# Attention feeding a soft mixture of experts: two sums on VectorE change places with a maximum

## Chip, cores and metric

The kernel runs on one core of a Trainium2 chip. The time is device microseconds of one execution; a comparison uses the median of several runs. The engines are named as in the profile: PE is TensorE's matmuls, PEld its weight loads, DVE VectorE, ACT ScalarE, POOL GpSimd, SP SyncE, whose queue issues the DMAs. `L67` stands on every row because one helper records every operation; rows are told apart by the tiles they write and read (`out<-in`).

## What is computed

Causal attention over 8 batches and 12 heads (448 positions, head dimension 64), and its output, one row of 768 numbers for each of 3584 positions, goes through a soft mixture of 8 experts with 4 slots each.

```python
scores = np.where(mask, -1e9, scale * q @ k.T)
attn = np.exp(scores - scores.max(-1)); attn /= attn.sum(-1) + 1e-9
x = attn @ v                                     # all heads side by side: (3584, 768)
logits = x @ phi                                 # (3584, 32)
d = np.exp(logits - logits.max(0)); d /= d.sum(0) + 1e-9
slot_input = d.T @ x                             # "dispatch": over all positions
slot_out[e] = np.maximum(slot_input[e] @ w1[e], 0) @ w2[e]
c = np.exp(logits - logits.max(1)); c /= c.sum(1) + 1e-9
out = c @ slot_out                               # "combine"
```

The maximum over positions and the sum over positions in `d` run over the whole input, so the kernel carries a running maximum, a running sum and a running dispatch result that is rescaled (`si = si * al + new`).

## The kernel before

**Stages.** A head is one of 96, a pair `p` is two heads of one batch, and a batch is six pairs. The main loop has one turn `block(p)` (lines 570 to 677) for each of pairs 0 to 45; line 681 does the last pair in another order; then the rest of the mixture (two weight matrices for each expert, streamed from memory, and the combine) follows as a tail. `a = 2 * p` is the first head of the pair, `m6 = p % 6` the pair's place in its batch.

**One head.** Its scores lie in a PSUM tile `s` of 128 x 1024 fp32, columns given by `SCOL` (line 50): the four blocks of keys start at columns 576, 0, 320 and 512. There are three such tiles, used in turn (`s_[i % 3]`).
- `scores1` (line 259) writes the causal mask by a matmul with the identity (the rows `s<-tri,identb`) and adds the products of q and k. The mask part `c03`, first of all, goes to columns 512 to 703; the part `c12` (256 columns) comes after it.
- `max_keys` (line 289) takes, on DVE, maxima over the keys into the small tile `r`; `max_row(i, 0)` turns them round on PE (`rt`, or `s<-ident,r` when the target is a score tile), and `max_row(i, 1)` (line 319) reduces the turned tile on DVE into `mr`.
- `max_spread` (line 324) spreads `mr` on POOL into the tile `r2` (the rows `r<-mr`).
- `scores2` (line 335), the correction, subtracts the maxima by a matmul with `r2` (the rows `s<-r,k`); it also carries the low parts of q and k, which POOL prepares with two subtractions, `sub_k` (`ks<-kraw,ks`) and `sub_q` (`r<-qraw,qd`).
- `exps` on ACT makes `pt` from the whole tile `s`; `attv_pair` multiplies by v into `po`, and `norm` on DVE divides by the sums and writes `x`.

**One turn.** In PE's order: correction of head a, `scores1` of head a + 2, correction of head a + 1, `scores1` of head a + 3, `attv_pair(p)` with the turning of head a + 2's maxima in its middle, then what the mixture needs, the turning of head a + 3's maxima, and the turning of the pair before's `x` (`xm`). POOL's order in a turn: the spread for head a + 1 (issued at the end of the turn before), `sub_k`, `sub_q`, the spread for head a + 2.

**What the mixture adds.** It uses the free score tile `m = s_[(a + 1) % 3]` (line 649), which the next turn's `scores1` takes again.
- In turns with m6 = 1, 3 or 5 (from p = 3 on) `logits_a` multiplies two pairs' turned `x` by phi into columns 0 to 127, and `logits_t` (line 444) adds that to the running tile `lt` on DVE (`lt<-s,lt`, `lt<-s,mk`).
- In turns with m6 = 3, 4 or 0 (from p = 9 on) `dispatch_a` multiplies a finished batch's `x` by its weights `gs` into 128 columns from 512, 256 columns from 512, or 384 columns from 0, and `dispatch_b` (line 486) adds that to `si` on DVE (`si<-si,al,s`), scaled by `al`, which ACT makes in the turn with m6 = 3.
- In turns with m6 = 2 `logits_e` copies two tiles out on DVE (`gs<-s`, `lg<-s`).
- In every turn the second head's maxima are turned into the last 128 columns of the same tile, 896 to 1023 (line 664), and reduced from there (`mr<-s`).

**Order of the work.** It is written by hand. Every operation goes through the helper `_InOrder` (line 57), which keeps each engine's instructions in the order of the program; between engines the framework puts the waits that the tiles ask for. So what stands behind a waiting instruction on its engine waits too.

Of the kernel before, what the change touches and what calls it, by code (L numbers as in the profile page):

```python
# [17 lines left out]
P = 128  # L18
# [64 lines left out]
def attention_soft_moe(ctx: ExitStack, tc: tile.TileContext, qk, va, phi, w, out):  # L83
# [52 lines left out]
    def loads_v(p, eng=nc.sync):  # L136
        if p < NPAIR:
            eng.dma_start(out=va_[p % 2], in_=va[p])
# [30 lines left out]
    def load_w(n):  # L169
        if n < len(order):  # L170
            t = wtiles[order[n]] = slot(n, f"w{n}")
            q, g, c = place(n), (n + 2) // 4, WN * ((n + 2) % 4)
            if n < RES or n == NBUF or q >= RES + LATE2:
                nc.sync.dma_start(out=t, in_=w[g, :, c:c + WN])
            elif 4 <= q < RES and n > NBUF:
                if q % 4 == 3:
                    nc.sync.dma_start(out=group(n), in_=w[g])
            elif n % 2:
                t = group(n)
                nc.sync.dma_start(out=t[:, 2 * WN:] if q < RES else t, in_=w[g, :, c - WN:c + WN])  # L180
# [39 lines left out]
    def misc(name):  # L220
        return ps_1.tile([P, 512], F32, tag="m", name=name)
# [13 lines left out]
    def cast_q(p, hs=slice(0, 2)):  # L235
        if p < NPAIR:
            nc.scalar.activation(out=qd[:, hs], in_=st["raw", 0, p][:, hs], func=AF.Copy)
# [10 lines left out]
    def copy_k2(p, hs=slice(0, 2)):  # L248
        if p < NPAIR:
            nc.scalar.activation(out=heads(k2_)[64:P, hs, 0:S], in_=kv(p)[0:64, hs],  # L250
                                 func=AF.Copy)
# [58 lines left out]
    def max_row(i, k, w=RW - RF, to=None):  # L310
        if i >= NHD:
            return
        if k == 0:
            st["rt", i] = misc(f"rt{i}") if to is None else to
            if w == AW:
                nc.tensor.matmul(st["rt", i][0:w, 0:P], r_[i % 2][:, RF:RF + w], ident, start=True, stop=True)
            else:
                nc.tensor.transpose(out=st["rt", i][0:w, 0:P], in_=r_[i % 2][:, RF:RF + w], identity=ident)
        else:
            mr = st["mr", i] = wk.tile([NQB, 32], F32, tag="mr", name=f"mr{i}", bufs=2)  # L320
            nc.vector.tensor_reduce(out=mr, in_=st.pop(("rt", i))[0:NQB, 0:P].rearrange("p (g t)->p t g", g=4),
                                    axis=AX.X, op=ALU.max, negate=True)
# [12 lines left out]
    def scores2(i, cs):  # L335
        if i >= NHD:
            return
        p, h = divmod(i, 2)
        s = st["s", i]
        k2 = k2_  # L340
        for c in cs:
            o, w, m = KS * h + P * c, S - CQ0[c], min(P, KS - P * c)
            nc.tensor.matmul(s[0:m, SCOL[c]:SCOL[c] + w], k2[:, o:o + m],
                             r2[:, h, CQ0[c]:S], start=False, stop=True, skip_group_check=True)

    def exps(i):
        if i < NHD:
            nc.scalar.activation(out=pt_[i % 2][:, 0:1024], in_=st.pop(("s", i)), func=AF.Exp, scale=SCALE)
# [56 lines left out]
    def norm(p, k):  # L405
        if k == 0:
            sm = st["sm", p] = moe.tile([P, NQ], F32, tag="sm", name=f"sm{p}", bufs=2)
            nc.vector.tensor_scalar(out=sm, in0=po2[:, :, HD], scalar1=EPS, scalar2=None, op0=ALU.add)
        elif k == 1:
            nc.vector.reciprocal(out=st["sm", p], in_=st["sm", p])  # L410
        else:
            x, sm = x_of(p), st.pop(("sm", p))
            m = NCH - 1
            nc.vector.tensor_tensor(out=x[:, 0:m].rearrange("p c (h d)->p h c d", h=2),
                                    in0=po2[:, 0:2 * m, 0:HD].rearrange("p (h c) d->p h c d", h=2),
                                    in1=sm[:, 0:2 * m].rearrange("p (h c)->p h c", h=2).unsqueeze(3)
                                    .to_broadcast([P, 2, m, HD]), op=ALU.mult)
            for h in range(2):
                a = AW * h
                nc.vector.tensor_scalar(out=x[0:AW, m, HD * h:HD * h + HD], in0=po2[a:a + AW, 2 * m, 0:HD],  # L420
                                        scalar1=sm[a:a + AW, 2 * m:2 * m + 1], scalar2=None, op0=ALU.mult)
# [22 lines left out]
    def logits_t(j, g):  # L444

        nc.vector.tensor_tensor(out=lt, in0=g, in1=lt if j else mk, op=ALU.add)
# [39 lines left out]
    def dispatch_b(b, hf, sp, sl=slice(0, 384)):  # L486
        s = si[:, 384 * hf + sl.start:384 * hf + sl.stop]
        nc.vector.scalar_tensor_tensor(out=s, in0=s, scalar=st["al", b][:, 0:1], in1=sp[:, 0:sl.stop - sl.start],
                                       op0=ALU.mult, op1=ALU.add)
# [80 lines left out]
    def block(p):  # L570
        a, b = 2 * p, p // 6 - 1
        m6 = p % 6
        if p + 1 < NPAIR:
            loads_v(p + 1, nc.sync if p + 1 < NPAIR - 1 else nc.scalar)
        if p % 2 and p < 44 or p in (16, 30):
            load_w(st["w"])
            st["w"] += 1

        if p:
            norm(p - 1, 2)  # L580
        scores2(a, range(NCH))
        exps(a)
        if p == 0:
            copy_k2(0, h1)
            cast_q(1, h1)
            warm(START[3], pob)
            max_row(1, 0)
            max_row(1, 1)
            max_spread(1)
            sub_k(1, h1, nc.vector)  # L590
        elif p > 1:
            xcopy(p - 2)
        scores1_all(a + 2)
        if p == 0:
            warm(START[2], pob)
        for k in range(3):
            max_keys(a + 2, k)
        if p == 0:
            cast_k(2, h0)
        scores2(a + 1, range(NCH))  # L600
        exps(a + 1)
        if p == 0:
            cast_k(2, h1)
        scores1_all(a + 3)
        if m6 == 2 and p > 6:
            logits_b(b)
        max_keys(a + 3, 0)
        late_k = p == 1
        if p == 1:
            sub_q(2, h0)  # L610
            sub_k(3, h0)
            sub_q(2, h1)
            load_qk(4, 0)
        elif p:
            sub_k(p + 2, h0 if late_k else slice(0, 2))
            if not late_k:
                load_qk(p + 4, 1)
            sub_q(p + 1)
            load_qk(p + 3, 0)
        else:  # L620
            sub_q(1, h0)
            sub_q(1, h1)
            load_qk(3, 0)
            sub_k(2, h0)
        copy_k2(p + 1)
        if m6 == 2 and p > 6:
            logits_d(b, lt)
        if p:
            cast_k(p + 3)
            cast_q(p + 2)  # L630
        else:
            cast_q(2)
            cast_k(3)
        if m6 == 3 and p > 6:
            logits_al(b)
        elif m6 == 4 and p > 6:
            logits_n(b)
        attv_pair(p)
        max_row(a + 2, 1)
        max_spread(a + 2)  # L640
        if p == 0:
            sub_k(2, h1)
            load_qk(4, 1)
        for k in (1, 2):
            max_keys(a + 3, k)
        for k in range(2):
            norm(p, k)

        m = s_[(a + 1) % 3]
        parts = []  # L650
        if m6 in (1, 3, 5) and p > 1:
            j = (m6 + 3) % 6
            logits_a(b if m6 == 1 else p // 6, (j, j + 1), m[:, 0:P])
        elif m6 == 2 and p > 6:
            logits_e(b, m, 0)
        if m6 == 3 and p > 6:
            parts = [(b, 0, slice(0, P), 512)]
        elif m6 == 4 and p > 6:
            parts = [(b, 0, slice(P, 3 * P), 512)]
        elif m6 == 0 and p > 6:  # L660
            parts = [(b - 1, 1, slice(0, 3 * P), 0)]
        for d, hf, sl, o in parts:
            dispatch_a(d, hf, m[:, o:o + sl.stop - sl.start], sl)
        max_row(a + 3, 0, to=m[:, 1024 - P:1024])
        max_row(a + 3, 1)
        if m6 == 2 and p > 6:
            logits_e(b, m, 1)
        max_spread(a + 3)
        if late_k:
            sub_k(p + 2, h1)  # L670
            load_qk(p + 4, 1)
        if m6 in (1, 3, 5) and p > 1:
            logits_t(j, m[:, 0:P])
        for d, hf, sl, o in parts:
            dispatch_b(d, hf, m[:, o:o + sl.stop - sl.start], sl)
        if p:
            xtrans(p - 1)

# [7 lines left out]
    i, b, p = NHD - 1, NB - 1, NPAIR - 1  # L686
# [62 lines left out]
    parts = [(hf, slice(a, a + 192)) for hf in range(2) for a in (0, 192)]  # L749
# [256 lines left out]
```

## Time and profile before

| | us |
|---|---|
| median of 3 runs (lowest, highest) | 396.44 (396.0, 397.08) |
| the profiled execution's own time | 395.86 |
| its span in the trace | 394.1 |
| main loop and last pair, up to about | 302 |
| tail (experts and combine) | 92 |

PE is busy 365.4 us of the span, DVE 294.9, ACT 283.0, POOL 256.6 (all of POOL's work lies in the loop). The granted TensorE clock is full in the loop. One cycle of six turns, a batch, takes 36.2 to 36.3 us. A row of the timeline reads: start, duration, engine, line, operation, tiles out<-in, shapes, count, and in brackets the engine's idle time before it with what ended it by the profile. A row with a count over 1 is several instructions merged, with the time from the first's start to the last's end. A matmul row gives the modelled end. The instruction named after an arrow is the one that ended last by the profile and need not be the one that was waited for.

### The profile page before, as it was taken

The numbers are of one execution on the slowest core, as the hardware profiler recorded it, in microseconds if no ns is written. First come the engines' busy times: TensorE is split into PE (matmuls) and PEld (weight loads), VectorE is DVE, ScalarE is ACT, GpSimd is POOL, SyncE is SP. The second block draws the span as 40 slices with busy tenths as digits, with TensorE's granted clock in tenths as the row PEclk, the third lists the DMA queues.
The fourth block names the chain that finished last, engine by engine and source line by source line (L and its number), as shares of the span: only waits on it lengthen the run. The fifth ranks groups of instructions, "written<-read, shape, count | busy, mean of one in ns | idle before, by whom it ended". The sixth has DMA issues, their size and how long they took to land.

```text
span 394.1 us, 14000 instructions
## 1 busy us (share of the span) xinstructions
PE 365.4 (93%) x5766; PEld 293.3 (74%) x5766; DVE 294.9 (75%) x835; ACT 283.0 (72%) x397; POOL 256.6 (65%) x214
## 2 busy tenths in 40 slices
PE   7899999999999999999999999999999998997840
PEld 3689889888988998898889888988986544533420
DVE  7787889888888888898888988888885575433540
ACT  5888889888898898888988989888864011432430
POOL 5998889888898888898988988889861000000000
PEclk9999999999999999999999999999999999999995
DMA  7858887778898788787987876887579999999997
GB/s 259 306 194 283 293 285 247 254 256 276 286 312 275 239 276 284 254 248 266 318 308 235 307 238 244 279 283 258 176 250 374 414 438 425 429 423 415 430 433 324
DMA packets 28720, 119.17 MB, mean 302 GB/s; under 512 B 3440, under 2 KB 3952, under 8 KB 26480
## 3 DMA queue, kind: packets, MB, share of 16 engines
q1 hardware_dynamic: 28512, 118.01, 82.9%
q8 instruction: 45, 0.74, 0.7%
q10 hardware_dynamic: 144, 0.27, 0.2%
q14 instruction: 19, 0.16, 0.1%
HBM read 107.25 MB, written 11.01 MB: 300 GB/s over the span
## 4 chain that ended last, share of the span: by engine, by line
PE 64%; DMA 11%; POOL 9%; DVE 6%; ACT 4%; issue 2%; SPq 0%; POOLq 0%; DVEq 0%; ACTq 0%
PE s L67 35%; PE po L67 20%; DMA w<-in_w_dram 9%; POOL r L67 6%; PE xm L67 4%; POOL ks L67 3%; DVE lm L67 2%; PE rt L67 2%; DMA kraw<-in_qk_dram 2%; DVE lg L67 1%; ACT qd L67 1%; PE pp L67 1%; PE e L67 1%; DVE si L67 1%; ACT w L67 1%
## 5 line engine op out<-in xcount | busy, mean ns | idle before, releaser
L67 DVE TRANSPOSE_TENSOR_REDUCE r<-s 128x32 f32<-128x1024 f32 x96 | 119.5, 1245 | 7.4 <-PE s L67 4.7
L67 ACT ACTIVATE pt<-s 128x1024 f32<-128x1024 f32 x96 | 98.7, 1029 | 30.8 <-PE s L67 22.5
L67 PEld LDWEIGHTS po<-va,pt 128*64 128x64 f32 x3040 | 103.6, 138 | 12.0 <-issue 11.5
L67 PE MATMUL po<-va,pt 128*64 128x65 f32 x3040 | 110.6, 224 | 0.0
L67 POOL TENSOR_TENSOR r<-qraw,qd 64x896 fp32r<-64x896 f32 (+1 forms) x49 | 99.3, 2027 | 3.2 <-ACT qd L67 1.8
L67 POOL TENSOR_TENSOR ks<-kraw,ks 64x896 fp32r<-64x896 f32 (+1 forms) x48 | 89.7, 1870 | 4.1 <-ACT ks L67 0.4
L67 POOL TENSOR_SCALAR_AFFINE_SELECT r<-mr 14x448 fp32r<-14x448 f32 x96 | 61.8, 644 | 31.9 <-DVE mr L67 27.2
L67 PE MATMUL s<-qd,ks 128*66 128x64 f32 (+3 forms) x384 | 80.2, 320 | 0.0
L67 PE MATMUL s<-r,k 128*128 128x448 f32 (+3 forms) x384 | 65.1, 291 | 3.1 <-POOL r L67 3.1
L67 PEld LDWEIGHTS s<-r,k 128*128 128x128 f32 (+1 forms) x384 | 59.3, 175 | 8.8 <-POOL r L67 6.6
L67 PEld LDWEIGHTS s<-qd,ks 128*128 128x128 f32 (+1 forms) x384 | 52.1, 182 | 2.0 <-issue 0.9
L67 ACT ACTIVATE ks<-kraw 128x896 fp32r<-128x896 f32 (+1 forms) x49 | 45.0, 920 | 5.3 <-DMA kraw<-in_qk_dram 4.1
L67 ACT ACTIVATE k<-ks 64x896 fp32r<-64x896 f32 (+1 forms) x49 | 45.8, 935 | 1.2
L67 ACT ACTIVATE qd<-qraw 128x896 fp32r<-128x896 f32 (+1 forms) x48 | 44.7, 931 | 1.3 <-POOL r L67 0.7
L67 PE MATMUL s<-tri,identb 128*128 128x192 bf16 x192 | 39.2, 268 | 0.6
L67 DVE TENSOR_REDUCE r<-r 128x16 f32<-128x32 f32 x192 | 33.7, 176 | 5.0
L67 DVE TENSOR_REDUCE mr<-s 14x32 f32<-14x128 f32 x47 | 13.1, 279 | 21.9 <-ACT qd L67 14.1
L67 PE MATMUL xm<-ident,x 128*128 128x128 f32 x188 | 28.3, 273 | 0.0
L67 ACT ACTIVATE xts<-xm 128x512 f32<-128x512 f32 x46 | 27.1, 590 | 0.0
L67 DVE TENSOR_SCALAR x<-po,sm 64x64 f32<-64x64 f32 x94 | 26.0, 276 | 0.7
L67 DVE TENSOR_TENSOR x<-po,sm 128x384 f32<-128x384 f32 x47 | 25.2, 537 | 0.0
L67 DVE COPY w<-pp 128x384 f32<-128x384 f32 x28 | 14.4, 553 | 13.2 <-PE pp L67 13.1
(148 smaller groups left out, 393.6 us busy)
## 6 DMA issues: line engine op xcount, KB each, us to landing
w<-in_w_dram SPq DMA_DIRECT2D x34, 768.0 KB, 6.6
kraw<-in_qk_dram SPq DMA_DIRECT2D x46, 448.0 KB, 4.3
qraw<-in_qk_dram SPq DMA_DIRECT2D x46, 448.0 KB, 4.5
w<-in_w_dram SPq DMA_DIRECT2D x5, 3072.0 KB, 23.9
va<-in_va_dram SPq DMA_DIRECT2D x47, 260.0 KB, 4.9
out_dram<-w SPq DMA_DIRECT2D x7, 1536.0 KB, 13.3
w<-in_w_dram SPq DMA_DIRECT2D x5, 1536.0 KB, 9.9
qk<-in_qk_dram SPq DMA_DIRECT2D x2, 448.0 KB, 7.2
```

The costliest lines, as they stand in the source:

```text
L67: return self._tc.keep_in_program_order(op(*args, **kwargs))
```

## The change

In `block(p)`, two calls move up on DVE: `logits_t` (m6 = 1, 3, 5) and `dispatch_b` (m6 = 3, 4, 0) are called between the turning of the second head's maxima on PE and their reduction on DVE, where they were called behind that reduction and its spread. No operation is added or dropped.

```diff
         for d, hf, sl, o in parts:
             dispatch_a(d, hf, m[:, o:o + sl.stop - sl.start], sl)
         max_row(a + 3, 0, to=m[:, 1024 - P:1024])
+        if m6 in (1, 3, 5) and p > 1:
+            logits_t(j, m[:, 0:P])
+        for d, hf, sl, o in parts:
+            dispatch_b(d, hf, m[:, o:o + sl.stop - sl.start], sl)
         max_row(a + 3, 1)
         if m6 == 2 and p > 6:
             logits_e(b, m, 1)
@@
         if late_k:
             sub_k(p + 2, h1)
             load_qk(p + 4, 1)
-        if m6 in (1, 3, 5) and p > 1:
-            logits_t(j, m[:, 0:P])
-        for d, hf, sl, o in parts:
-            dispatch_b(d, hf, m[:, o:o + sl.stop - sl.start], sl)
         if p:
             xtrans(p - 1)
```

## The prediction

> **What bounds the kernel now.** I read the page first, then the waits, then the engines' timelines over one full cycle of six turns of the loop (a turn is one call of `block(p)`; turns 22 to 27 start at 143.2, 149.3, 155.3, 161.4, 167.6 and 173.3 us).
>
> ```profile
> PE 365.4 (93%) x5766; PEld 293.3 (74%) x5766; DVE 294.9 (75%) x835; ACT 283.0 (72%) x397; POOL 256.6 (65%) x214
> ```
> ```profile
> POOL r L67 <- DVE mr L67: 27.2, 41, 1.2
> ```
>
> TensorE (PE) is busy 93% of the span, so the loop can only get longer through a wait of PE. The second row says where PE's nearest rival sits: GpSimd (POOL) spends its idle time waiting for the maxima `mr` that VectorE (DVE) makes, 27.2 us in 41 waits. One turn of POOL, turn 25:
>
> ```profile
> 161.70 0.64 POOL L67 TENSOR_SCALAR_AFFINE_SELECT r<-mr 14x448 fp32r<-14x448 f32 x1 [0.68 <-DVE mr L67]
> 162.42 1.94 POOL L67 TENSOR_TENSOR ks<-kraw,ks 64x896 fp32r<-64x896 f32 x1
> 164.33 2.11 POOL L67 TENSOR_TENSOR r<-qraw,qd 64x896 fp32r<-64x896 f32 x1
> 166.51 0.64 POOL L67 TENSOR_SCALAR_AFFINE_SELECT r<-mr 14x448 fp32r<-14x448 f32 x1
> ```
>
> After its one wait POOL has no gap over 0.1 us. It spreads the second head's maxima (161.70), does the two subtractions, and spreads the next first head's maxima (166.51 to 167.15). So if the spread at 161.70 starts late, the one at 166.51 is late by as much. PE needs both: the first for the second correction of that turn, the second for the first correction of the next turn.
>
> **The change, part by part.** Nothing is added or removed. On DVE the logits sum `lt` (turns with p mod 6 = 1, 3, 5) and the dispatch sum `si` (p mod 6 = 3, 4, 0) go from behind `mr` to in front of it. PE, ACT, POOL and SP keep their order and no DMA is moved. DVE now, at the ends of turns 21, 22 and 24:
>
> ```profile
> 143.16 0.28 DVE L67 TENSOR_REDUCE mr<-s 14x32 f32<-14x128 f32 x1 [0.73 <-ACT qd L67]
> 143.37 0.27 DVE L67 TENSOR_TENSOR lt<-s,mk 128x128 f32<-128x128 f32 x1
> 143.57 0.33 DVE L67 SCALAR_TENSOR_TENSOR si<-si,al,s 128x128 f32<-128x128 f32 x1
> 143.83 0.54 DVE L67 TENSOR_TENSOR x<-po,sm 128x384 f32<-128x384 f32 x1
> ...
> 149.23 0.28 DVE L67 TENSOR_REDUCE mr<-s 14x32 f32<-14x128 f32 x1 [0.51 <-ACT qd L67]
> 149.44 0.46 DVE L67 SCALAR_TENSOR_TENSOR si<-si,al,s 128x256 f32<-128x256 f32 x1
> 149.83 0.54 DVE L67 TENSOR_TENSOR x<-po,sm 128x384 f32<-128x384 f32 x1
> ...
> 161.35 0.28 DVE L67 TENSOR_REDUCE mr<-s 14x32 f32<-14x128 f32 x1 [0.72 <-ACT qd L67]
> 161.56 0.59 DVE L67 SCALAR_TENSOR_TENSOR si<-si,al,s 128x384 f32<-128x384 f32 x1
> 162.08 0.54 DVE L67 TENSOR_TENSOR x<-po,sm 128x384 f32<-128x384 f32 x1
> ```
>
> Start to start, a place in DVE's queue costs 0.20 us for `lt`, 0.26, 0.39 and 0.52 us for `si` of 128, 256 and 384 columns, 0.21 us for `mr`. DVE sits idle 0.51 to 0.73 us before `mr`, so all depends on whether the sums can run in that gap. Their products are finished before the transposes for `mr`, but does their wait end there? The next rows say no.
>
> ```profile
> 161.96 0.10 PEld L67 LDWEIGHTS <-identb 128*128 128x128 bf16 x1
> 162.21 0.24 PE L67 MATMUL s<-tri,identb 128*128 128x192 bf16 x1
> ```
>
> This mask matmul of turn 25 has its weights at 161.96 and starts at 162.21, right behind the dispatch sum (161.56 + 0.59 = 162.15). But it writes columns 512 to 703 of the score tile (`c03`), while that sum reads columns 0 to 383. So the program's waits go by the whole tile. The transposes write columns 896 to 1023 of the same tile and are issued before the sums; the sums must then wait for them as `mr` does, and start only where `mr` starts now. Hence each sum put in front makes `mr` later by its full place: 0.46 us (0.20 + 0.26) at the end of p mod 6 = 3, 0.39 at 4, 0.20 at 5, 0.52 at 0, 0.20 at 1, nothing at 2. `si` also waits for `al`, which is no later:
>
> ```profile
> 142.96 0.28 ACT L67 ACTIVATE al<-run_m,run_m 128x1 f32<-128x1 f32 x1
> ```
>
> It ends at 143.24, before 143.16 + 0.20 = 143.36. Nothing is won in exchange: the tile is freed when the last of the same DVE instructions ends, 161.56 + 0.59 = 162.15 now and 161.35 + 0.52 + 0.28 = 162.15 afterwards; the work behind (`x<-po`) starts as before.
>
> **What the lateness meets.** Behind `mr` stand the spread and POOL's whole turn; ACT's `qd` and the loads of q and k follow POOL too, and their slack I take as enough. The slack is read from the ends of POOL's spreads to the starts of PE's corrections:
>
> ```profile
> 143.51 0.64 POOL L67 TENSOR_SCALAR_AFFINE_SELECT r<-mr 14x448 fp32r<-14x448 f32 x1 [0.92 <-DVE mr L67]
> 148.31 0.64 POOL L67 TENSOR_SCALAR_AFFINE_SELECT r<-mr 14x448 fp32r<-14x448 f32 x1
> 154.38 0.64 POOL L67 TENSOR_SCALAR_AFFINE_SELECT r<-mr 14x448 fp32r<-14x448 f32 x1
> 160.38 0.64 POOL L67 TENSOR_SCALAR_AFFINE_SELECT r<-mr 14x448 fp32r<-14x448 f32 x1
> 172.64 1.43 POOL L67 TENSOR_SCALAR_AFFINE_SELECT r<-mr 14x448 fp32r<-14x448 f32 x2
> ```
> ```profile
> 144.65 0.63 PE L67 MATMUL s<-r,k 128*128 128x448 f32 x4
> 149.28 0.72 PE L67 MATMUL s<-r,k 128*128 128x448 f32 x4
> 155.29 0.71 PE L67 MATMUL s<-r,k 128*128 128x448 f32 x4
> 155.84 0.26 PE L67 MATMUL s<-tri,identb 128*128 128x192 bf16 x1
> 161.41 0.71 PE L67 MATMUL s<-r,k 128*128 128x448 f32 x4
> 162.91 0.63 PE L67 MATMUL s<-r,k 128*128 128x448 f32 x4
> 163.37 0.26 PE L67 MATMUL s<-tri,identb 128*128 128x192 bf16 x1
> 167.55 0.71 PE L67 MATMUL s<-r,k 128*128 128x448 f32 x4
> 173.33 0.73 PE L67 MATMUL s<-r,k 128*128 128x448 f32 x4
> 173.91 0.26 PE L67 MATMUL s<-tri,identb 128*128 128x192 bf16 x1
> ```
>
> At 173.33 PE already waits: the spread ends at 172.64 + 0.64 = 173.28, and the signal costs 0.05. A correction that waited costs 0.03 more (next mask 0.58 after it at 173.33, 0.55 at 155.29). So a slack is the distance less 0.08. At the ends of turns 22 to 26: 149.28 - 148.95 - 0.08 = 0.25; 155.29 - 155.02 - 0.08 = 0.19; 161.41 - 161.02 - 0.08 = 0.31; 167.55 - 167.15 - 0.08 = 0.32; and 0. Within a turn, before the second correction: 144.65 - 144.15 - 0.08 = 0.42 in turn 22, and 162.91 - 162.34 - 0.08 = 0.49 in turn 25; elsewhere I take it as not deciding.
>
> **The sum.** POOL's lateness in a turn is PE's at the transposes before it plus the delay of `mr`; PE's is the largest of what it had and POOL's less the slack.
> - Turn 22: POOL 0.46 late, PE 0.04 after the second correction (0.46 - 0.42). Turn 23 starts 0.46 - 0.25 = 0.21 late.
> - Turn 23: POOL 0.04 + 0.39 = 0.43. Turn 24 starts 0.43 - 0.19 = 0.24 late.
> - Turn 24: POOL 0.21 + 0.20 = 0.41, less 0.31 is under 0.24. Turn 25 starts 0.24 late.
> - Turn 25: POOL 0.24 + 0.52 = 0.76; second correction 0.76 - 0.49 = 0.27 late; turn 26 starts 0.76 - 0.32 = 0.44 late.
> - Turn 26: POOL 0.27 + 0.20 = 0.47, no slack: turn 27 starts 0.47 late. Turn 27 gets nothing more, since the end of turn 26 is not changed.
>
> So 0.47 us a cycle, and turns 9 to 44 are six cycles: 2.8 us. Before turn 9 only `lt` is moved, at the ends of turns 3, 5 and 7, and it hits turns that end like this, with no slack:
>
> ```profile
> 40.34 0.65 POOL r L67
> 41.04 2.71 PE s L67 x20
> ```
>
> 40.99 + 0.05 = 41.04: 0.20 late, three times, 0.6 us. Together 3.4 us. The tail follows the loop's end, and I let it move as a whole. The profiled execution took 395.86 us (span 394.1 and 1.76 around it), so 399.3 for one like it; it lies 0.58 below the median of 396.44, so on the median 399.8 us. The bounds of this sum: if POOL had no slack anywhere, every delay would land on PE, 6 x (0.46 + 0.39 + 0.20 + 0.52 + 0.20) + 0.6 = 11.2 us; if the sums ran wholly in DVE's gap, 0 or a little less. I stay by the measured slacks; an error of 0.1 in each of two deciding ones moves the sum by 1.2.
>
> **Rivals.**
> *Waits by halves of the tile.* The sums of columns 0 to 511 would wait for their own products alone.
>
> ```profile
> 160.13 0.85 PE L67 MATMUL s<-x,gs 128*32 128x384 f32 x8
> 160.91 0.30 PE L67 MATMUL s<-ident,r 128*76 128x128 f32 x1
> ```
>
> The transposes end at 161.21 and are seen at 161.35, 0.14 later. So the 384-column sum would start at 160.98 + 0.14 = 161.12 and `mr` at 161.64, 0.29 late, not 0.52; `lt` would cost nothing; the sums of turns 21 and 22, in the other half, delay `mr` by 0.39 (from `al`'s end) and 0.39. The cycle runs 0.14, 0.20, 0.20, then 0.20 + 0.29 - 0.32 = 0.17 and stays there: 1.0 us in six cycles, none before, 397.4 us. The Trainium skill, "PSUM — Partial Sum Buffer", section "PSUM bank collisions raise a hardware error", asks that PSUM be guarded by bank and quadrant, not by address, and a bank there is 2 KiB, half this tile; by that rule this would be the time, 397.4 us. The row at 162.21 speaks against it here, since that wait crosses the halves.
>
> *The wait holds back the weight load too.* Before the second correction the load starts 0.20 us ahead of its matmul:
>
> ```profile
> 162.71 0.68 PEld L67 LDWEIGHTS s<-r,k 128*128 128x128 f32 x4
> ```
>
> If POOL's signal holds that load and the lead is needed, the slack within a turn falls by some 0.2 us, which makes the second corrections of turns 23 and 25 the deciding ones: about 0.4 a cycle more, 2.4 us, 402.3 us. For it: the load at 173.33 starts only with its matmul. Against: that start cost 0.03, not 0.2.
>
> *Faster: the sums run in DVE's gap and POOL's lateness is hidden.* The score tile is then free sooner. In turn 25 the mask matmul could start up to 0.25 earlier, but the second mask waits for the exponential:
>
> ```profile
> 162.16 1.03 ACT L67 ACTIVATE pt<-s 128x1024 f32<-128x1024 f32 x1 [0.86 <-DVE si L67]
> ```
>
> It ends at 163.19, so 163.37 can come forward to 163.24, 0.13; turn 22 gives 0.05. 6 x 0.18 = 1.1 us, 395.3 us. It decides from the point where the slack at a turn's end exceeds the delay of `mr`; 0.25 and 0.19 against 0.39 speak against it.
>
> **How the numbers follow.** Forecast 0.66, the weight load 0.14, waits by halves 0.14, hidden lateness 0.06. A measurement of this kernel tells some 0.3% (1.2 us) from no change. The first two are slower: 0.80. Halves (1.0 us) is within the bound, and the last (1.1 us) lies at it and is shared out: same 0.17, faster 0.03. The range runs from the halves' time, a little under it, to the load's, a little over: 397.0 to 402.8 us; the forecast's own is 398.6 to 401.0.
>
> **What would show it.** In the profile after: `lt` or `si` starts where `mr` started, about 0.44 us after the transposes' start, with `mr` 0.2 to 0.5 us later; POOL's wait for `mr` grows; PE's load waits for POOL's `r` in several turns of each cycle instead of one, and a cycle takes 36.7 us instead of 36.2. If the sums start 0.2 us before the old place of `mr`, the waits are not by tile and the forecast is too slow; if the gaps stand before the second corrections, it is too fast; if the cycle is unchanged though `mr` is late, POOL's slack was misread.

## The result, and the profile after

| | before | after |
|---|---|---|
| median (lowest, highest), us | 396.31 (396.0, 397.08) | 399.59 (399.28, 399.84) |
| runs | 4 | 4 |
| the profiled execution's own time, us | 395.86 | 399.84 |
| its span, us | 394.1 | 398.1 |

The ratio is 1.0076, 95% interval 1.0064 to 1.0088: 3.28 us slower. The forecast was 399.8 us, slower. All medians and ratios leave out three executions in a slow state: 1176.81 us of the kernel before, and 443.9 and 761.67 us of the second kernel with small instructions in DVE's gap. The instructions of every engine but DVE stand in the same order as before; on DVE `mr` has changed places with `lt` and `si`, and nothing else.

The busy times of the engines in the changed kernel, from its page:

```profile
PE 368.4 (93%) x5766; PEld 291.6 (73%) x5766; DVE 295.1 (74%) x835; ACT 285.6 (72%) x397; POOL 256.2 (64%) x214
```

The work is what it was (PE 365.4 us before, POOL 256.6). The waits of the changed kernel, as engine and tile, what ended the wait, us in total, times, longest:

```profile
POOL r L67 <- DVE mr L67: 29.5, 37, 1.5
...
PEld s L67 <- POOL r L67: 9.4, 28, 1.2
```

and the second of these before:

```profile
PEld s L67 <- POOL r L67: 6.6, 15, 1.2
```

POOL waits 2.3 us more for the maxima (27.2 before), and PE's loads wait for POOL's spread 28 times instead of 15, 2.8 us more. DVE in the changed kernel, at the ends of turns 21, 22 and 24 (turns 22 to 27 start at 144.97, 151.17, 157.21, 163.36, 169.65 and 175.46 us here):

```profile
144.88 0.29 DVE L67 TENSOR_TENSOR lt<-s,mk 128x128 f32<-128x128 f32 x1 [0.70 <-ACT qd L67]
...
145.35 0.27 DVE L67 TENSOR_REDUCE mr<-s 14x32 f32<-14x128 f32 x1
...
150.97 0.48 DVE L67 SCALAR_TENSOR_TENSOR si<-si,al,s 128x256 f32<-128x256 f32 x1 [0.47 <-PE s L67]
151.37 0.27 DVE L67 TENSOR_REDUCE mr<-s 14x32 f32<-14x128 f32 x1
...
163.28 0.61 DVE L67 SCALAR_TENSOR_TENSOR si<-si,al,s 128x384 f32<-128x384 f32 x1 [0.69 <-ACT qd L67]
163.81 0.27 DVE L67 TENSOR_REDUCE mr<-s 14x32 f32<-14x128 f32 x1
```

DVE's idle gap is still there (0.70, 0.47, 0.69 us), and the sums stand behind it, not in it. POOL's spreads of the same cycle in the changed kernel:

```profile
145.69 0.64 POOL L67 TENSOR_SCALAR_AFFINE_SELECT r<-mr 14x448 fp32r<-14x448 f32 x1 [1.34 <-DVE mr L67]
...
150.48 0.64 POOL L67 TENSOR_SCALAR_AFFINE_SELECT r<-mr 14x448 fp32r<-14x448 f32 x1
...
156.52 0.64 POOL L67 TENSOR_SCALAR_AFFINE_SELECT r<-mr 14x448 fp32r<-14x448 f32 x1
...
162.35 0.64 POOL L67 TENSOR_SCALAR_AFFINE_SELECT r<-mr 14x448 fp32r<-14x448 f32 x1
164.15 0.64 POOL L67 TENSOR_SCALAR_AFFINE_SELECT r<-mr 14x448 fp32r<-14x448 f32 x1 [1.16 <-DVE mr L67]
...
168.95 0.64 POOL L67 TENSOR_SCALAR_AFFINE_SELECT r<-mr 14x448 fp32r<-14x448 f32 x1
...
174.76 1.43 POOL L67 TENSOR_SCALAR_AFFINE_SELECT r<-mr 14x448 fp32r<-14x448 f32 x2
```

And PE in the changed kernel: the starts of turns 9, 22 and 45, and between them the cycle of turns 22 to 27:

```profile
65.49 0.70 PE L67 MATMUL s<-r,k 128*128 128x448 f32 x3
...
144.97 0.71 PE L67 MATMUL s<-r,k 128*128 128x448 f32 x4
146.38 0.74 PE L67 MATMUL s<-r,k 128*128 128x448 f32 x4
151.17 0.73 PE L67 MATMUL s<-r,k 128*128 128x448 f32 x4
157.21 0.73 PE L67 MATMUL s<-r,k 128*128 128x448 f32 x4
162.87 0.30 PE L67 MATMUL s<-ident,r 128*76 128x128 f32 x1
163.36 0.72 PE L67 MATMUL s<-r,k 128*128 128x448 f32 x4
164.84 0.73 PE L67 MATMUL s<-r,k 128*128 128x448 f32 x4
169.65 0.73 PE L67 MATMUL s<-r,k 128*128 128x448 f32 x4
175.46 0.73 PE L67 MATMUL s<-r,k 128*128 128x448 f32 x4
181.62 0.60 PE L67 MATMUL s<-r,k 128*128 128x448 f32 x2
...
285.42 0.74 PE L67 MATMUL s<-r,k 128*128 128x448 f32 x4
```

Hold the two lists side by side. Spread ends and correction starts are 151.12 and 151.17, 157.16 and 157.21, 162.99 and 163.36, 169.59 and 169.65; at the end of turn 26 the first of the two merged spreads ends at 175.40, and the correction starts at 175.46. So PE starts on POOL's signal at the ends of turns 22, 23, 25 and 26, and not at that of turn 24. Within a turn the spreads that end at 146.33 (turn 22) and 164.79 (turn 25) are followed by corrections at 146.38 and 164.84. Before, the end of turn 26 was the only such place in this cycle.

The same starts before:

```profile
64.49 0.73 PE L67 MATMUL s<-r,k 128*128 128x448 f32 x4
...
143.22 0.72 PE L67 MATMUL s<-r,k 128*128 128x448 f32 x4
...
179.49 0.72 PE L67 MATMUL s<-r,k 128*128 128x448 f32 x4
...
282.21 0.73 PE L67 MATMUL s<-r,k 128*128 128x448 f32 x4
```

This cycle took 36.27 us before (179.49 - 143.22) and takes 36.65 now. Turns 9 to 44 took 217.72 and take 219.93 us, so 2.21 more; turns 1 to 8 took 47.80 and take 48.25, so 0.45 more. That is 2.66 us in the turns. The other 1.3 of these two profiles' difference (398.1 - 394.1 = 4.0) lies ahead of turn 1 (0.55) and behind the start of turn 45 (111.9 and 112.7, 0.75); of the medians' 3.28 us it is 0.6. Turn 1 started between 16.66 and 17.59 us in the profiles of all twelve kernels of this study, though they do the same up to there, so the stretch ahead of it says nothing about the change.

For the experiments I use the length of a turn, from one first correction to the next, as a mean over the six turns with the same m6 among turns 9 to 44 (worked out from PE rows like those above):

| m6 of the turn | 0 | 1 | 2 | 3 | 4 | 5 | turns 9 to 44 | turns 1 to 8 |
|---|---|---|---|---|---|---|---|---|
| before | 6.129 | 6.140 | 5.784 | 6.162 | 6.067 | 6.006 | 217.72 | 47.80 |
| after | 6.152 | 6.271 | 5.828 | 6.163 | 6.202 | 6.039 | 219.93 | 48.25 |
| growth | 0.02 | 0.13 | 0.04 | 0.00 | 0.14 | 0.03 | 2.21 | 0.45 |
| only the logits sum moved | 6.130 | 6.140 | 5.943 | 6.161 | 6.035 | 6.006 | 218.50 | 48.23 |
| only the dispatch sum moved | 6.159 | 6.269 | 5.692 | 6.220 | 6.116 | 6.143 | 219.59 | 47.73 |

Turn 22 has m6 = 4, turn 25 has m6 = 1.

### The profile page after: what moved, and what is told of

Read it like the earlier page. It is cut to its first block, busy times and chain, and to the rows that moved or that the text cites. A ratio compares the mean times of both kernels' runs of the same rounds, so it can differ in the third digit from the quotient of the medians.

```text
span 398.1 us, 14000 instructions
## 1 busy us (share of the span) xinstructions
PE 368.4 (93%) x5766; PEld 291.6 (73%) x5766; DVE 295.1 (74%) x835; ACT 285.6 (72%) x397; POOL 256.2 (64%) x214
## 4 chain that ended last, share of the span: by engine, by line
PE 62%; POOL 11%; DMA 10%; DVE 7%; ACT 4%; issue 2%; SPq 0%; POOLq 0%; DVEq 0%; ACTq 0%
PE s L67 34%; PE po L67 19%; DMA w<-in_w_dram 9%; POOL r L67 8%; PE xm L67 4%; POOL ks L67 3%; DVE lm L67 2%; ACT qd L67 2%; DMA qraw<-in_qk_dram 1%; DVE lg L67 1%; PE pp L67 1%; DVE si L67 1%; PE rt L67 1%; PE e L67 1%; ACT w L67 1%
## 5 line engine op out<-in xcount | busy, mean ns | idle before, releaser
L67 PE MATMUL po<-va,pt 128*64 128x65 f32 x3040 | 109.4, 223 | 0.0
L67 PE MATMUL s<-r,k 128*128 128x448 f32 (+3 forms) x384 | 67.2, 297 | 3.6 <-POOL r L67 3.4
L67 PEld LDWEIGHTS s<-r,k 128*128 128x128 f32 (+1 forms) x384 | 57.6, 175 | 13.8 <-POOL r L67 9.4
L67 ACT ACTIVATE xts<-xm 128x512 f32<-128x512 f32 x46 | 27.2, 592 | 0.0
L67 ACT ACTIVATE w<-pp 128x384 f32<-128x384 f32 x28 | 12.5, 490 | 15.5 <-PE pp L67 15.4
```

Source lines behind the costliest of these rows:

```text
L67: return self._tc.keep_in_program_order(op(*args, **kwargs))
```

## The experiments

### Each sum by itself

The logits sum alone is moved up:

```diff
         max_row(a + 3, 0, to=m[:, 1024 - P:1024])
+        if m6 in (1, 3, 5) and p > 1:
+            logits_t(j, m[:, 0:P])
         max_row(a + 3, 1)
```

> Only the logits sum goes ahead of the second head's maxima (turns with p mod 6 = 1, 3, 5); the dispatch sum keeps its old place. Theory (the sums wait for the whole tile, the maxima are late by their place on VectorE, and GpSimd passes that on where it has no slack): maxima 0.17 to 0.20 us late at the ends of these turns. The recurrence of the prediction with these delays alone gives 1.5 (0.17) to 1.75 us (0.20), so some 397.9 us against 396.3, a loss mostly at turns that end without slack (p = 4, 6, 8 and p mod 6 = 2). Rival, waits by halves of the tile: the logits lie in the other half than the transposes, nothing is late, 396.3 us.

The dispatch sum alone is moved up:

```diff
         max_row(a + 3, 0, to=m[:, 1024 - P:1024])
+        for d, hf, sl, o in parts:
+            dispatch_b(d, hf, m[:, o:o + sl.stop - sl.start], sl)
         max_row(a + 3, 1)
```

> Only the dispatch sum goes ahead (p mod 6 = 3, 4, 0); the logits sum keeps its old place. Theory: 0.24, 0.37 and 0.50 us late; the recurrence gives 2.0 to 2.4 us, 398.5 us. Alone the two parts sum to more than both together (3.5 against the measured 3.3 and the loop's 2.7), since GpSimd's lateness is not added up from turn to turn: the larger counts. Rival, waits by halves: 0.9 us, 397.2 us, with the 384-column sum starting some 0.2 us before the old place of the maxima.

Measured beside each other and 396.84 us for the kernel before: 398.38 us (ratio 1.0038, 1.0026 to 1.0051) for the logits sum, 399.0 us (1.0057, 1.0044 to 1.0070) for the dispatch sum; 1.54 and 2.16 us more.

The places of the loss tell more than its size. `lt` alone makes `mr` 0.18 us later at the ends of turns with m6 = 1, 3 and 5, but of the turns behind these only m6 = 2 became longer, 5.784 to 5.943 us; 4 and 0 did not (6.035 and 6.130). Of the three, only the turns with m6 = 2 have no slack at their end.

In the early turns, where only `lt` is moved, turns 4, 6 and 8 grew, and turns 1 to 8 together by 0.43 us, as in the changed kernel (0.45); without `lt` moved they did not (47.73).

With the dispatch sum alone the loss of turn 22 (m6 = 4) mostly goes: 6.116 us, where it was 6.067 before and 6.202 in the changed kernel. The loss appears in the turn behind (m6 = 5, 6.143 instead of 6.006 before), where 0.37 of delay meets a slack of 0.19. The first sum is a special case here. Without `lt` in front of it, it waits for `al`:

```profile
144.63 0.35 DVE L67 SCALAR_TENSOR_TENSOR si<-si,al,s 128x128 f32<-128x128 f32 x1 [0.77 <-ACT al L67]
```

So `mr` is 0.31 us late at the ends of turns with m6 = 3, not the 0.24 that I had expected, and a little over the prediction's slack of 0.25. Yet the spread that turn 23 needs still ends 0.09 us ahead of its correction (150.02 + 0.64 = 150.66 and 150.75), where a correction that waits follows by 0.05: that slack was read too small. What turn 22 does lose, 0.05, comes from the score tile: its last reader `lt` ends later, and the mask matmul starts 0.78 us behind the correction (145.42 - 144.64) instead of 0.73 (143.95 - 143.22). The turns with m6 = 2 even became shorter (5.692 from 5.784): they end on POOL's signal, and POOL is less late there than PE at their start.

The two effects do not add up (1.54 + 2.16 = 3.70 us, together 3.28). By the working of the prediction that is because they use the same slack; the medians alone, each known to some 0.5 us, could not show it.

### What the sums wait for

Both sums are called ahead of the transposes, so they wait for their own products alone; if waits go by the whole tile, the transposes must then wait for the sums.

```diff
+        if m6 in (1, 3, 5) and p > 1:
+            logits_t(j, m[:, 0:P])
+        for d, hf, sl, o in parts:
+            dispatch_b(d, hf, m[:, o:o + sl.stop - sl.start], sl)
         max_row(a + 3, 0, to=m[:, 1024 - P:1024])
         max_row(a + 3, 1)
```

> The order on VectorE of the changed kernel, with the two sums called ahead of the transposes of the second head's maxima instead of behind them: each engine has the same instructions in the same order as in the changed kernel, only the direction of the wait between the sums and the transposes turns round. Theory, waits by the whole tile: now the transposes on TensorE wait for the sums to have read, about 0.54 us in turns with p mod 6 = 1 and 5, 0.96 at 3, 0.73 at 4 and 0.86 at 0, some 3.4 us a cycle and 22 us in all: 418 us. Waits by halves: only the sums in the upper half (p mod 6 = 3 and 4) hold the transposes, 1.7 us a cycle, 406 us. Waits by columns: no wait, about 396 us.

Measured: 419.17 us in one execution, against 396.54 before; the rows of its profile decide here. PE and DVE of this kernel at the end of a turn with only the logits in it:

```profile
178.33 0.29 DVE L67 TENSOR_TENSOR lt<-s,lt 128x128 f32<-128x128 f32 x1 [0.27 <-PE s L67]
...
178.68 0.30 PE L67 MATMUL s<-ident,r 128*76 128x128 f32 x1 [0.48 <-DVE lt L67]
```

The transposes write columns 896 to 1023, the sum reads columns 0 to 127, in the other half of the tile, and still they start 0.06 us after its end (178.62). In this program the wait goes by the tile. So waits by halves are out, and in the changed kernel, where the transposes come first in the program, the sums wait for them.

### Lateness without a sum, and how much DVE's gap holds

The order of before, with instructions put ahead of `mr` that wait for nothing (a small tile multiplied by one, in place); by the forecast they run in DVE's idle gap, `mr` is not late, and nothing is lost.

```diff
+        if p > 1 and m6 != 2:
+            for _ in range({1: 2, 5: 2, 3: 4, 4: 3, 0: 4}[m6] if p > 6 or m6 % 2 else 0):
+                nc.vector.tensor_scalar(out=mk, in0=mk, scalar1=1.0, scalar2=None, op0=ALU.mult)
         max_row(a + 3, 1)
```

> The kernel before with two to four extra VectorE operations put ahead of the second head's maxima in every turn where the change puts a sum there. They multiply the constant mask tile mk (128 x 128) by one, touch no score tile and wait for nothing. Theory: they run in the 0.5 to 0.7 us in which VectorE sits idle for the transposes, the maxima are at most as late as the part that does not fit, and the time stays at 396.3 us (within 0.5). Rival, it is the place in VectorE's queue that costs, whatever stands there: about 399.6 us like the change.

Measured: 402.72 us, against 396.54 (ratio 1.0153, 1.0139 to 1.0167). The expectation failed: I took the instructions for shorter than they are. DVE of this kernel at the ends of turns 23 and 24:

```profile
157.77 0.71 DVE L67 TENSOR_SCALAR mk<-mk 128x128 f32<-128x128 f32 x2
...
163.69 1.34 DVE L67 TENSOR_SCALAR mk<-mk 128x128 f32<-128x128 f32 x4
```

Four of them took 1.34 us, twice the gap: the first 0.56 beside a spread of POOL (more on this in the last section), the others 0.23 each. Behind two of them (0.71 us, about the gap) the turns kept their length, m6 = 0 and 2 with 6.131 and 5.774 us; behind three or four, m6 = 1, 4 and 5 grew by 0.45, 0.21 and 0.23 us. `mr` was late by 0.46, 0.22 and 0.24 us there. But PE did not lose this time to POOL. PE in turn 25 of this kernel, and from its list of waits the two that bear on it (engine and tile, what ended the wait, us in total, times, longest):

```profile
165.79 0.24 PE L67 MATMUL s<-tri,identb 128*128 128x192 bf16 x1 [0.53 <-DVE si L67]
```
```profile
PEld s L67 <- POOL r L67: 6.5, 15, 1.2
PE s L67 <- DVE si L67: 6.0, 19, 0.6
```

The waits for POOL are those of before (6.6, 15 times). What is new is the other row: here the sums still stand behind the late `mr`, so the score tile is free later, and the mask matmul waits 0.53 us for `si`. So this kernel shows a second path on which a late `mr` costs time, and says nothing for the first. The changed kernel does not pay on it: its mask matmul of turn 25 starts 0.77 us behind the correction (164.13 - 163.36), and before it was 0.80 (162.21 - 161.41).

So the same with one or two of them:

```diff
-            for _ in range({1: 2, 5: 2, 3: 4, 4: 3, 0: 4}[m6] if p > 6 or m6 % 2 else 0):
+            for _ in range({1: 1, 5: 1, 3: 2, 4: 1, 0: 2}[m6] if p > 6 else m6 % 2):
```

> As the run with extra VectorE operations that wait for nothing, but shorter: one took 0.33 us there, so one is put ahead of the second head's maxima in turns with p mod 6 = 1, 5 and 4 (0.33 us) and two in turns with 3 and 0 (0.66 us). That is 0.9 to 1.7 times the length of what the change puts there, and less than VectorE's idle time of 0.51 and 0.72 us at these places. Theory: all of it runs while VectorE would sit idle, the maxima are not late, 396.4 us, within 0.4 us of the kernel before. Rival, a place in VectorE's queue costs by itself: 399 to 400 us.

Measured: 396.79 us, against 396.54 (1.0010, 1.0000 to 1.0019); all mean turn lengths but one are those of before within 0.01 us. That one (m6 = 2, 5.832) comes from turn 44 alone, 0.34 us longer, behind a `mr` that started 0.36 us late though the small instruction had ended; why it did I have not found. DVE of this kernel at the ends of turns 23 and 25:

```profile
154.54 0.46 DVE L67 TENSOR_SCALAR mk<-mk 128x128 f32<-128x128 f32 x1
155.14 0.28 DVE L67 TENSOR_REDUCE mr<-s 14x32 f32<-14x128 f32 x1
...
166.81 0.33 DVE L67 TENSOR_SCALAR mk<-mk 128x128 f32<-128x128 f32 x1
```

Work ahead of `mr` costs nothing as long as it may start in the gap. What costs is that the sums may not.

### Taking away POOL's load

If the loss is POOL's lateness, it should go when POOL has slack. Both kernels here leave out the second head's half of `sub_k` (the low part of k), so their output is not the reference's; POOL's subtraction then takes 1.14 us instead of 1.94 (the row at 162.02 below).

```diff
-            sub_k(p + 2, h0 if late_k else slice(0, 2))
+            sub_k(p + 2, h0)
```

The kernel before with this edit:

> The kernel before, with the subtraction that makes the low parts of k done for the first head of each pair only in the turns from p = 2 on: half of that GpSimd work is left out, so the second head's scores are less exact. GpSimd gets about 1 us of slack in every turn. Theory: the wait for GpSimd at the ends of turns with p mod 6 = 2 goes (0.1 to 0.2 us a cycle), 395 to 396 us. It is the base for the next run.

The changed kernel with this edit:

> The changed kernel with the same half of the subtraction left out. Theory: the maxima are as late as in the changed kernel, but GpSimd's turn ends 1 us earlier, so nothing is late at the ends of turns; only the second corrections within a turn can wait, 0.01 to 0.04 us in turns with p mod 6 = 4, 5 and 1: at most 0.5 us over the same edit on the kernel before. Rivals that do not go through GpSimd's turn (VectorE itself, the release of the score tile, the start or the tail): the whole 3.3 us stays.

Measured: 395.73 us (ratio to the whole kernel before 0.9968, 0.9956 to 0.9980) and 396.38 us (0.9986, 0.9977 to 0.9995). The change of order costs 0.65 us here, where it costs 3.28 with all of POOL's work; turns 9 to 44 take 217.50 and 218.00 us. DVE, POOL and PE around turn 25 of the second kernel, a fence for each:

```profile
160.43 0.61 DVE L67 SCALAR_TENSOR_TENSOR si<-si,al,s 128x384 f32<-128x384 f32 x1 [0.69 <-ACT qd L67]
160.96 0.27 DVE L67 TENSOR_REDUCE mr<-s 14x32 f32<-14x128 f32 x1
```
```profile
161.30 0.64 POOL L67 TENSOR_SCALAR_AFFINE_SELECT r<-mr 14x448 fp32r<-14x448 f32 x1 [1.73 <-DVE mr L67]
162.02 1.14 POOL L67 TENSOR_TENSOR ks<-kraw,ks 64x448 fp32r<-64x448 f32 x1
...
165.29 0.64 POOL L67 TENSOR_SCALAR_AFFINE_SELECT r<-mr 14x448 fp32r<-14x448 f32 x1
```
```profile
161.99 0.74 PE L67 MATMUL s<-r,k 128*128 128x448 f32 x4
...
166.69 0.72 PE L67 MATMUL s<-r,k 128*128 128x448 f32 x4
```

`mr` is as late as in the changed kernel (0.53 us behind the start of `si`), but the spread for the next turn ends at 165.93, 0.76 ahead of its correction. What stays is the second correction of the same turn (161.94 and 161.99), which less work behind it can't help: turns with m6 = 1 and 4 are 0.03 us longer than in the kernel beside it, and those with m6 = 5 0.02. I had expected 0.5 us at most. So the path of most of the loss is `mr`, POOL's turn, PE.

### Looking for a faster order

Two kernels make `mr` earlier by turning the second head's maxima into a small tile of their own, ahead of the products; the first for m6 = 0 and 3, the second for all m6 but 2.

```diff
+        early_row = p > 6 and m6 in (0, 3)      # the second kernel: p > 6 and m6 != 2
+        if early_row:
+            max_row(a + 3, 0)
         m = s_[(a + 1) % 3]
...
-        max_row(a + 3, 0, to=m[:, 1024 - P:1024])
+        if not early_row:
+            max_row(a + 3, 0, to=m[:, 1024 - P:1024])
```

> The kernel before, but in turns with p mod 6 = 0 and 3 (from p = 9 on) the second head's maxima are turned into the small PSUM tile that the first head's use, and before the mixture's products instead of behind them; the sums stay behind the maxima. Theory: the maxima are ready 0.7 us earlier, GpSimd's spread 0.6 us, the sums wait for their products alone and the score tile is free some 0.25 and 0.18 us sooner in the next turns, of which 0.13 and 0.06 us reach the end of the turn (the second mask waits for the exponential): 1.1 us gained, 395.2 us. Rival, the transposes of x now wait for the maxima (they share the small tile): up to 0.3 us lost in each such turn, 397 to 399 us.

> The same in all turns with p mod 6 other than 2 from p = 9 on. Theory: in turns with p mod 6 = 1, 4 and 5 the products are short, so that the transposes of x wait for the maxima by some 0.13 us each (0.4 us a cycle); gained are 0.2 us as in the run with 0 and 3 alone and 0.17 us from GpSimd's wait at the ends of turns with p mod 6 = 2: near nothing in all, 396 to 396.6 us.

Measured: 397.59 us (1.0023, 1.0013 to 1.0032) and 400.28 us (1.0093, 1.0080 to 1.0107), against 396.54. Both expectations failed; the first kernel's time lies where its rival had it (397 to 399 us). In the first, the turns behind (m6 = 1 and 4) became shorter, by 0.21 and 0.14 us, and more than expected, but the turns themselves (0 and 3) became longer, by 0.19 and 0.22. PE at the end of turn 24 of the first:

```profile
161.22 0.28 PE L67 MATMUL rt<-ident,r 128*76 128x128 f32 x1
161.43 0.85 PE L67 MATMUL s<-x,gs 128*32 128x384 f32 x8
...
162.63 0.71 PE L67 MATMUL s<-r,k 128*128 128x448 f32 x4
```

and the one row of before that the prediction does not show there, behind the transposes of 160.91:

```profile
161.05 0.60 PE L67 MATMUL xm<-ident,x 128*128 128x128 f32 x4
```

From the first of these matmuls to the correction it is 1.41 us; before, products first, it was 161.41 - 160.13 = 1.28, so 0.13 of the loss is here. The products start 0.21 us after the transposes, where `xm` followed them by 0.14. The rival was that `xm` waits for `mr`. By the profile its loads do, 3.8 us in 6 waits in the first kernel and 9.2 us in 26 in the second; but in turn 24 of the first `xm` starts 0.79 us behind the products (162.22 - 161.43), and before what followed them started 0.78 behind (160.91 - 160.13), so there the wait costs next to nothing. The two orders differ in how often matmuls of 76 and of 32 columns of weights change over. The Trainium skill, "TensorEngine Tiling (Array Packing)", section "Key Properties", states that a change of tiling mode drains TensorE. The rows agree with that as far as they go (0.21 against 0.14 us), but no run here takes the change of shape by itself, so this is argued and not shown; the rest of the loss of these turns (0.06 and 0.09 us) I have not located.

The last kernel gives DVE a piece of POOL's work in its gap: 96 of 448 columns of `sub_k` for turns 4, 6 and, from 8 on, those with m6 = 2.

```diff
-            sub_k(p + 2, h0 if late_k else slice(0, 2))
+            if shared(p):                        # p in (4, 6) or p > 7 and p % 6 == 2
+                sub_k_part(p + 2)                # POOL: columns 0 to 351
+            else:
+                sub_k(p + 2, h0 if late_k else slice(0, 2))
...
+        if shared(p + 1):
+            ks = kv(p + 3)[64:P, :, S - KD:S]    # KD = 96
+            nc.vector.tensor_tensor(out=ks, in0=st["raw", 1, p + 3][64:P, :, S - KD:S], in1=ks, op=ALU.subtract)
         max_row(a + 3, 1)
```

> The other way round: work that waits for nothing is taken from GpSimd and put into the idle time of VectorE ahead of the second head's maxima. In turns p = 4, 6 and in those with p mod 6 = 2 from p = 8 on, which end without slack on GpSimd, 96 of the 448 columns of the low parts of k are subtracted by VectorE at the end of the turn before; GpSimd does the other 352 (0.4 us less). Theory: turns 4 and 6 become 0.4 us shorter, turn 8 0.2 us (the run with half the subtraction left out showed 5.35, 5.35 and 5.59 us for these), the later ones gain 0.2 us of which the next turn gives most back (ScalarE's cast of q comes last there): 1.0 to 1.2 us in all, 395.2 us. Rival, VectorE and GpSimd slow each other or the subtraction delays the maxima: no gain, 396.3 us or more.

Measured: 395.94 us, against 396.54 (0.9985, 0.9977 to 0.9994). It is the fastest whole kernel here, by 0.6 us where I had expected 1.0 to 1.2, and its interval ends just under 1. In turn 4 POOL's subtraction took 1.57 instead of 1.94 us. Turns 4, 6 and 8 fell from 5.79 to 5.37, 5.46 and 5.66 us, the later turns with m6 = 2 from 5.784 to 5.585; but those with m6 = 3 rose by 0.14. So most of the gain of a cycle is given back in the turn behind. PE's loads at the start of turn 27 of this kernel show which wait takes it:

```profile
173.90 0.14 PEld L67 LDWEIGHTS s<-qd,ks 128*66 128x66 f32 x1 [0.16 <-ACT qd L67]
```

PE comes earlier to the products of q and k, and waits for ACT's cast of q, which ends at 173.86 us: six such waits, 1.0 us in all, none of them before. The expectation had named this wait.

## Why the prediction was right

**What the sums wait for.** Right. They start with the transposes done, 163.28 - 162.87 = 0.41 us after their start, and the kernel with the sums ahead of the transposes shows the wait by the whole tile (178.62, 178.68). The rival by halves of the tile (397.4 us) is out; its sum was a little small besides, since by the prediction's own rule PE keeps the 0.20 that it had, which gives 1.2 us and not 1.0. The rule that the prediction named beside it (the Trainium skill, "PSUM — Partial Sum Buffer", "PSUM bank collisions raise a hardware error"), by bank and quadrant, does not say how the waits of this program are set: by the measurement they are wider than a bank.

**How late `mr` is.** A little too large. The prediction took each delay as a full place in DVE's queue. But where `mr` started 0.44 us after the transposes before (161.35 - 160.91), the first sum starts 0.41 after them (163.28 - 162.87) and `mr` 0.94 (163.81 - 162.87), so at the end of turn 24 it is 0.50 late and not 0.52. The means over turns 9 to 44 are 0.43, 0.37, 0.18, 0.50 and 0.18 at the ends of turns with m6 = 3, 4, 5, 0 and 1.

**Slack and where PE waits.** Right at all points of the cycle: the ends of turns 22, 23, 25 and 26 and the second corrections of turns 22 and 25 wait for POOL, the end of turn 24 does not. Turn by turn the prediction had turns 22 to 27 longer by 0.21, 0.03, 0, 0.20, 0.03 and 0; the means of six are 0.14, 0.03, 0.02, 0.13, 0.04 and 0.00.

**The sum.** The mis-sized term is the cycle: 0.47 forecast, 0.37 measured (2.21 / 6; 0.38 in turns 22 to 27). With the measured delays its steps give: turn 23 starts 0.43 - 0.25 = 0.18 late, turns 24 and 25 0.01 + 0.37 - 0.19 = 0.19, turn 26 0.19 + 0.50 - 0.32 = 0.37, turn 27 0.20 + 0.18 = 0.38. Six cycles are 2.3, and the three early turns 3 x 0.18 = 0.5, so 2.8 us against 2.66 measured in the turns. Part of what is left is that POOL's way from `mr` to the end of the next spread is 0.01 to 0.03 us shorter a turn in the changed kernel, which adds to the slack. The forecast of 3.4 was 0.7 too large for the turns, and the median grew by 3.28 none the less, since 0.6 us came from outside them. That the total fits so well is partly luck. That the 0.6 us belongs to the change is not shown. The start scatters by 0.9 us over the twelve kernels; and in the changed kernel without half of `sub_k` turn 45 starts at 281.28 us, earlier than before (282.21), and what lies behind it still takes 112.7 us, as it does after the change.

**The weight load held back** (402.3 us) was right in its premise and wrong in what followed from it. The load of the second correction of turn 25 in the changed kernel:

```profile
164.84 0.59 PEld L67 LDWEIGHTS s<-r,k 128*128 128x128 f32 x4 [0.17 <-POOL r L67]
```

It waits for POOL's signal and starts with its matmul, which before it led by 0.20. The next mask matmul then starts 0.58 us behind that correction (165.42 - 164.84), before 0.46 (163.37 - 162.91): a second correction that waits costs some 0.1 us, not the 0.03 that the prediction took. But little of this reaches the end of the turn, where the transposes stand 5.66 us behind the first correction (169.02 - 163.36) instead of 5.64 (167.05 - 161.41). The load of turn 23's second correction, which this rival made a deciding one, waits too and leads by only 0.04 (152.41 and 152.45); but the mask matmul behind it starts where it did, 1.84 us after the first correction (153.01 - 151.17) and before 1.83, so it decides nothing either. **Hidden lateness** fell: at the ends of turns 22, 23, 25 and 26 the spreads end 0.05 us ahead of the corrections, so the delay is not hidden there.

**What the experiments add.** The forecast rested on slacks read from one cycle. The dispatch sum alone, which moves the loss from turn 22 to turn 23, and the logits sum alone, which costs only where the slack is nil, bear these out one by one, but for turn 22, whose slack was read some hundredths too small. Taking POOL's load away shows the path. What I misjudged afterwards was the price of filling the gap: independent instructions took about twice what I had taken for them, and the loss that followed went by the release of the score tile and not by POOL.

## What to carry to other kernels

An engine's idle gap can be filled only by what may start in it: read which instruction ends the gap, and whether the thing moved waits for the same event, by tiles as the program declares them, not by the columns that are touched. Where it does, each place given up on the way to a shared helper engine is paid at those turns where that engine has no slack left, so compare the end of its work with the start of its consumer turn by turn, and carry the lateness on. Ask also what stands behind the late instruction on its own engine: where that frees a buffer, the lateness is paid a second way. A busy share of 65% on POOL, or a gap of 0.7 us on DVE, says nothing about that.

## What was not expected of the hardware

The same small instruction on DVE (`mk<-mk`, 128 x 128, both in SBUF) had two durations. Of the kernel with one or two of them, all by tile (least, median, most ns):

```profile
L67 DVE TENSOR_SCALAR mk<-mk x48: 176/322/540, 34.5 to 294.0; 128x128 f32<-128x128 f32 x48
```

and POOL's spreads beside the two shown above:

```profile
154.28 0.64 POOL L67 TENSOR_SCALAR_AFFINE_SELECT r<-mr 14x448 fp32r<-14x448 f32 x1
...
166.42 0.64 POOL L67 TENSOR_SCALAR_AFFINE_SELECT r<-mr 14x448 fp32r<-14x448 f32 x1
```

Apart from a spread it took 0.227 us (median of 14), together with one 0.370 (median of 34); the spreads kept their 0.64. Here the spreads end at 154.92 and 167.06 and the instruction at 155.00 and 167.14, both times 0.08 us later, though it began at different points of them (0.26 and 0.39 us in). In 31 of the 34 it ended 0.08 to 0.09 us after the spread; the other three began in the last 0.07 us of one and took 0.18. That looks like a wait for the spread's end. The Trainium skill, "SBUF — State Buffer", section "SBUF: two separate sides", states that VectorE and GpSimd share a pair of ports which one of them holds for a whole instruction while the other is fully blocked. It names the kinds of VectorE instruction that this meets; that this one is among them no run here shows. The two rows agree with the rule as far as they go.
